# Routing attention and a bilinear feed-forward block: the preparation of the last twelve head pairs put across by VectorE in 32 by 32 blocks

## The chip, the cores and the metric

One core of one Trainium2 chip runs the whole kernel in one launch. The metric is the device time of one execution in microseconds; less is better. The kernel before takes 1099.45 us (median of 3 runs, 1099.21 to 1100.14).

## What is computed

```python
# q, k, v: (4, 8, 768, 64); centroids: (8, 16, 64)
q_assign = argmax(einsum('bhsd,hcd->bhsc', q_n, c_n), axis=-1)   # k_assign alike
mask = q_assign[:, :, :, None] == k_assign[:, :, None, :]
scores = where(mask, matmul(q, k.T) / 8, -1e9)
attn = exp(scores - max) / (sum + 1e-9)
x = matmul(attn, v)                      # heads side by side: (3072, 512)
out = ((x @ w_a) * (x @ w_b)) @ w_out    # d_ff = 1536
```

Every query and key row gets the nearest of 16 centroids of its head; a query attends to the keys of its own cluster. The result goes through a bilinear feed-forward block.

## The kernel before

The 4 batch elements x 8 heads are worked off as 16 **pairs** of heads, p = 0 to 15, four to a batch element. `HP` is 4, so pairs 4 to 15 are those of the last three batch elements. A pair takes six **groups** (l = 0 to 5) of the loop at L891, and the loop index is g = 6p + l. In each group TensorE issues, in this order:

1. `score` of the group's two units (L408): one-hot clusters against one-hot clusters (L416) and q against k (L425) into the PSUM tiles `s`; ScalarE takes the exponential (L432).
2. `weigh` of the group before (L451): probabilities against v (L457).
3. one step of the **preparation of the next pair** (`ready[l]()`, L907, from `prep_steps`, L380).
4. in every third group `denominators` (L480).
5. pieces of the feed-forward block of an earlier batch element (the queue `ffn`, L928 to L937), as many as a credit in columns allows. In the later batch elements these are products of the up projections (L639) and of the down projection (L758), most of them followed by one or two VectorE additions (L649, L764). After each piece one entry of the queue `todo` is issued, a VectorE operation of the preparation or of the normalization (L499 to L515). What is left in `todo` follows at the group's end (L941).

All these products, and all transposes of the preparation, take turns in three PSUM tiles named `m` (pool `ps_m`, L172).

The preparation of pair p+1, spread over the groups of pair p, is:

- l = 0 and the end of l = 0: TensorE turns q and k, 12 transposes of 128 x 128 (L308), so that the head dimension lies across partitions; ScalarE copies them out of PSUM in three copies of 128 x 512 (L316).
- l = 1: similarities to the centroids (L324), copied to SBUF by ScalarE (L329). v of the pair is loaded (L215).
- l = 2: TensorE turns the similarities (three transposes, L335); VectorE finds the first largest of 16 in five operations (L352 to L358) and leaves one-hot rows in bf16.
- l = 4 and its end: TensorE turns the one-hot rows (12 transposes in bf16, L368), and ScalarE copies them out of PSUM in two copies of 128 x 768 (L373, L378). For k the copy makes 0 and -2^60 of 1 and 0.

At the end of group l = 0 the next q and k are requested from HBM (`load(p + 2)`, L947) by four DMAs on the SP queue, in runs of 256 bytes (L189). The SP queue works in order. It also carries the loads of w_a, w_b and w_out (L239, in the first 296 us) and the stores of the result (L529).

In groups 0 to 41 VectorE, ScalarE and GpSimd round the weights from 64-bit words to float32 (`round_w`, L244): four VectorE operations of 128 x 512, one each on ScalarE and GpSimd, and a last one on VectorE (L275), some 36 times.

A second path of the program (`long_path`) is taken only for out-of-range data and does not run here.

## Time and profile before

| | |
|---|---|
| median of 3 runs | 1099.45 us |
| the profiled execution's own time | 1098.49 us |
| its span, first to last instruction | 1096.7 us |
| TensorE busy | 1076.1 us (98%), granted clock 0.998 on the mean |
| VectorE busy | 683.8 us (62%) |
| GpSimd busy | 331.0 us (30%) |
| ScalarE busy | 303.4 us (28%) |
| DMA | 64,247 packets, 45.00 MB |

The profile shows one execution. PE is TensorE, PEld its weight loads, DVE VectorE, ACT ScalarE, POOL GpSimd, SPq the DMA issues of the SP queue. A float32 matmul of the program stands in the trace as two passes, a transpose as one. Matmuls overlap in the pipeline, so the duration of one is longer than the step from its start to the start of the next; the cost of a group of matmuls is read from start to start.

### The profile page before, as it was taken

What the parts mean: (1) busy time and instruction counts of PE and PEld (TensorE: products, weight loads), DVE (VectorE), ACT (ScalarE), POOL (GpSimd) and SP (SyncE); (2) the same over time, 40 slices, a digit from 0 to 9 for tenths busy, and PEclk for the clock granted to TensorE, in tenths of its full rate; (3) what the DMA queues carried; (4) which work ended last, traced back from release to release, by engine and by line L of the source; (5) the groups of instructions that cost most, each with busy time, mean ns of one, the idle gap of its engine ahead of it and who ended that gap; (6) DMA issues with size and microseconds to landing.
All of it is one profiled execution on the core that took longest, in us unless ns stands there. A gap on an engine that the chain in (4) does not pass through costs nothing.

```text
span 1096.7 us, 13426 instructions
## 1 busy us (share of the span) xinstructions
PE 1076.1 (98%) x5043; PEld 629.1 (57%) x5043; DVE 683.8 (62%) x1346; ACT 303.4 (28%) x572; POOL 331.0 (30%) x317
## 2 busy tenths in 40 slices
PE   6999999999999999999999999999999999999998
PEld 3444445555556765555455767555555678555687
DVE  5888767576747337566664735666566655676662
ACT  4656424443331322232222222222231210000000
POOL 1111243443441323434343232234344320121200
PEclk9999999999999999999999999999999999999999
DMA  5333242324201020101001020010000001000001
GB/s 151 94 92 83 63 116 90 108 77 120 77 22 32 15 58 20 44 1 44 1 1 44 19 59 15 13 40 1 15 1 1 5 20 34 1 0 1 1 25 36
DMA packets 64247, 45.00 MB, mean 41 GB/s; under 512 B 48816, under 2 KB 59568, under 8 KB 64176
## 3 DMA queue, kind: packets, MB, share of 16 engines
q1 hardware_dynamic: 63200, 42.22, 13.6%
q10 hardware_dynamic: 976, 1.87, 0.5%
q8 instruction: 41, 0.67, 0.2%
q14 instruction: 30, 0.25, 0.1%
HBM read 37.78 MB, written 6.29 MB: 40 GB/s over the span
## 4 chain that ended last, share of the span: by engine, by line
PE 89%; DVE 5%; issue 4%; POOL 1%; ACT 0%; DMA 0%; DVEq 0%; POOLq 0%
PE m L639 30%; PE m L758 16%; PE O L457 11%; PE m L539 11%; PE s L425 10%; PE s L416 3%; PE m L480 3%; PE m L308 2%; PE m L324 1%; PE m L368 1%; DVE raw L600 1%; POOL acc L446 1%; PE m L335 1%; DVE xT L600 0%; DVE acc L446 0%
## 5 line engine op out<-in xcount | busy, mean ns | idle before, releaser
L432 ACT ACTIVATE pt<-s 128x768 f32<-128x768 f32 x192 | 145.5, 809 | 242.5 <-PE s L425 196.0
L446 POOL TENSOR_TENSOR acc<-acc,pt 128x384 f32<-128x384 f32 x144 | 149.4, 1051 | 65.1 <-ACT pt L432 48.2
L654 POOL TENSOR_TENSOR h<-h,ha 128x384 f32<-128x384 f32 x72 | 72.8, 1020 | 261.0 <-DVE ha L649 258.3
L457 PE MATMUL O<-pt,v 128*64 128x384 f32 x768 | 145.1, 499 | 0.0
L425 PE MATMUL s<-qkT 64*128 64x384 f32 x768 | 140.7, 486 | 0.0
L649 DVE TENSOR_TENSOR ha<-ha,m 128x384 f32<-128x384 f32 x126 | 67.1, 548 | 86.1 <-PE m L639 85.3
L649 DVE TENSOR_TENSOR h<-h,m 128x384 f32<-128x384 f32 x126 | 67.5, 549 | 79.4 <-PE m L639 78.9
L457 PEld LDWEIGHTS O<-pt,v 128*64 128x64 f32 x768 | 46.6, 136 | 86.4 <-issue 83.7
L512 POOL TENSOR_TENSOR xT<-xT,acc 128x384 f32<-128x384 f32 x32 | 33.3, 1039 | 197.8 <-DVE acc L507 167.5
L446 DVE TENSOR_TENSOR acc<-acc,pt 128x384 f32<-128x384 f32 x96 | 71.7, 776 | 30.1 <-POOL acc L446 29.7
L425 PEld LDWEIGHTS s<-qkT 64*128 64x128 f32 x768 | 71.1, 189 | 32.0 <-issue 0.8
L758 PE MATMUL m<-wo_sb,h 128*128 128x256 f32 x384 | 87.1, 381 | 0.0
L758 PEld LDWEIGHTS m<-wo_sb,h 128*128 128x128 f32 x384 | 72.2, 190 | 13.6 <-issue 1.8
L639 PE MATMUL m<-raw 128*128 128x384 f32 x192 | 70.0, 487 | 0.0
L539 PE MATMUL m<-xT,wb_sb 128*128 128x384 f32 x192 | 66.7, 491 | 1.9 <-DVE h L554 1.9
L539 PE MATMUL m<-xT,wa_sb 128*128 128x384 f32 x192 | 66.9, 492 | 0.0
L758 PE MATMUL m<-xT,h 128*128 128x256 f32 x288 | 65.3, 382 | 0.1
L758 PEld LDWEIGHTS m<-xT,h 128*128 128x128 f32 x288 | 54.1, 190 | 11.1 <-DVE acc L507 1.8
L639 PE MATMUL m<-xT,wa_sb 128*128 128x384 f32 x144 | 52.9, 490 | 0.0
L639 PE MATMUL m<-xT,size 128*128 128x384 f32 x144 | 52.6, 488 | 0.0
L639 PE MATMUL m<-xT,wb_sb 128*128 128x384 f32 x144 | 52.6, 488 | 0.0
L539 PEld LDWEIGHTS m<-xT,wb_sb 128*128 128x128 f32 x192 | 35.5, 190 | 28.9 <-DVE h L554 3.7
(149 smaller groups left out, 1501.2 us busy)
## 6 DMA issues: line engine op xcount, KB each, us to landing
raw<-in_moe_w_out_dram SPq DMA_DIRECT2D x12, 512.0 KB, 3.2
qk<-in_q_dram SPq DMA_DIRECT2D x30, 192.0 KB, 3.7
qk<-in_k_dram SPq DMA_DIRECT2D x30, 192.0 KB, 4.1
v<-in_v_dram SPq DMA_DIRECT2D x15, 384.0 KB, 4.3
raw<-in_moe_w_a_dram SPq DMA_DIRECT2D x11, 512.0 KB, 3.5
raw<-in_moe_w_b_dram SPq DMA_DIRECT2D x11, 512.0 KB, 3.5
out_dram<-rest SPq DMA_DIRECT2D x24, 128.0 KB, 1.7
out_dram<-comb SPq DMA_DIRECT2D x12, 128.0 KB, 1.7
```

The source lines that it names most:

```text
L416: nc.tensor.matmul(out=s[:, a, 0:HB], lhsT=ohTs[p][r, S + j * P:S + (j + 1) * P], rhs=ohTs[p][r, hf * HB:(hf + 1) * HB], start=True, stop= ...
L425: nc.tensor.matmul(out=s[:, a, 0:HB], lhsT=qkTs[p][r, S + j * P:S + (j + 1) * P], rhs=qkTs[p][r, hf * HB:(hf + 1) * HB], start=False, stop ...
L432: nc.scalar.activation(out=pt, in_=s[:, :, 0:HB], func=AF.Exp, scale=SCALE)
L446: eng.tensor_tensor(out=acc[:, a, :], in0=probs[u - 1][:, a, :] if j == 1 else acc[:, a, :], in1=probs[u][:, a, :], op=ALU.add)
L457: nc.tensor.matmul(out=O_of[0][a * D:(a + 1) * D, 0:HB], lhsT=vs[p][:, a, j, :], rhs=probs[u][:, a, :], start=(j == 0), stop=(j == NJ - 1))
L480: nc.tensor.matmul(out=ps[a * D:(a + 1) * D, 0:HB], lhsT=ones, rhs=t[:, a, :], start=(n == 0), stop=(n == len(terms) - 1))
L512: nc.gpsimd.tensor_tensor(out=x, in0=x, in1=den, op=ALU.mult)
L539: nc.tensor.matmul(out=ps[:, 0:HB], lhsT=w_sb[:, ch, f * P:(f + 1) * P], rhs=xTs[b][:, ch, t0:t0 + HB], start=(ch == 0), stop=(ch == NCH - 1))
L639: nc.tensor.matmul(out=ps[:, 0:HB], lhsT=A[l][c], rhs=rhs[c], start=(c == 0), stop=(c == 1))
L649: nc.vector.tensor_tensor(out=out, in0=in0, in1=ps, op=op)
L654: nc.gpsimd.tensor_tensor(out=to, in0=to, in1=box[name], op=ALU.mult)
L758: nc.tensor.matmul(out=ps[:, 0:HN], lhsT=A[l][f // 3][:, f % 3, :], rhs=B[r][f // 2][:, f % 2, :], start=(f == 0), stop=(f == N2 - 1))
```

## The change

For pairs 4 to 15 (`by_blocks(p)`: p >= 4) TensorE turns nothing any more. VectorE's `transpose` works on each block of 32 x 32 by itself. The loads lay q and k out for it: partition 32n + t of `qk` holds the 32 head-dimension elements of half n of token 32j + t (n counts two heads and two halves of the head dimension). Two VectorE transposes of 128 x 768 then give the same `qkT` as before. The similarities stay in PSUM until a VectorE transpose of 128 x 384 takes them across; queries then lie in partitions 0 to 63, keys in 64 to 127. The last step of the one-hot is split: VectorE compares the query half, GpSimd subtracts in the key half (which gives 0 and at most -2^60 directly). One VectorE transpose of 128 x 384 in bf16 takes both across, and eight small DMAs on the SP queue put the rows where `score` reads them. Tokens now lie in natural order, so v comes in two DMAs with runs of 256 bytes and the stores of these batch elements use another row order.

```diff
-    ohtp = pool("ohtp", 2)
+    ohtp = pool("ohtp", 1)
...
+    def by_blocks(p):
+        return p >= HP
+
     def load(p):
...
+        if by_blocks(p):
+            t = qkp.tile([P, 2, S // 32, 32], FP32, name="qk")
+            for w, src in enumerate((q, k)):
+                for n in range(4):
+                    a, d = divmod(n, 2)
+                    nc.sync.dma_start(
+                        out=t[32 * n:32 * n + 32, w],
+                        in_=src[b, 2 * hp + a, :, 32 * d:32 * d + 32].rearrange(
+                            "(j t) d -> t j d", t=32))
+            qks[p] = t
+            return
...
+        if by_blocks(p):
+            for a in range(2):
+                nc.sync.dma_start(
+                    out=t[:, a], in_=v[b, 2 * hp + a].rearrange(
+                        "(j p) d -> p j d", p=P))
+            return
...
+    ohT_bufs = [ohtp.tile([P, 2 * S], BF16, name=f"ohT{n}") for n in range(2)]
+
+    rank_far = zero.tile([P, NC], FP32, name="rank_far")
...
+        if by_blocks(p):
+            sims[p] = ps
+            return
         t = simp.tile([P, HB], FP32, name="sim")
         nc.scalar.copy(out=t, in_=ps[:, 0:HB])
         sims[p] = t
...
+    def prep_by_blocks(p):
...
+        def across(w):
+            v.transpose(out=qkTs[p][:, w * S:(w + 1) * S],
+                        in_=qks[p][:, w].rearrange("p j d -> p (j d)"))
+
+        def sims_across():
+            v.transpose(out=sim.rearrange("p g c -> p (g c)"),
+                        in_=sims[p][:, 0:HB])
+
+        def one_hot():
+            nc.gpsimd.tensor_tensor(out=oh[KT], in0=sim[KT], in1=top(first)[KT],
+                                    op=ALU.subtract)
+            v.tensor_tensor(out=oh[QT], in0=sim[QT], in1=top(first)[QT],
+                            op=ALU.is_equal)
+
+        def one_hot_across():
+            v.transpose(out=ohT, in_=oh.rearrange("p g c -> p (g c)"))
+            for a in range(2):
+                for kq in range(4):
+                    r = 32 * kq + a * NC
+                    nc.sync.dma_start(
+                        out=ohTs[p][a * D:a * D + NC, kq * HB:(kq + 1) * HB],
+                        in_=ohT[r:r + NC, :])
+
+        return [
+            [lambda: across(0), lambda: across(1)],
+            [sims_across],
+            [lambda: v.tensor_reduce(out=mx, in_=sim, axis=AX.X, op=ALU.max),
+             lambda: v.tensor_tensor(out=sim, in0=sim, in1=top(mx), op=ALU.is_ge),
+             lambda: v.tensor_tensor(
+                 out=sim, in0=sim, in1=rank_far[:, None, :].broadcast_to(shape),
+                 op=ALU.mult),
+             lambda: v.tensor_reduce(out=first, in_=sim, axis=AX.X, op=ALU.max)],
+            [one_hot],
+            [one_hot_across],
+            [],
+        ]
...
+        if by_blocks(p):
+            steps = prep_by_blocks(p)
+            ready = [lambda s=s: todo.extend(s) for s in steps]
+            ready[1] = both(lambda: prep_sim(p), lambda: load_v(p), ready[1])
+            return ready
...
+    for r, factor in ((slice(0, P // 2), 1.0), (slice(P // 2, P), FAR)):
+        nc.vector.tensor_scalar(out=rank_far[r], in0=rank[r], scalar1=factor,
+                                scalar2=None, op0=ALU.mult)
...
         if l == 0 and p + 1 < NPAIR:
-            prep_transpose(p + 1, 2)
+            if not by_blocks(p + 1):
+                prep_transpose(p + 1, 2)
             load(p + 2)
-        if l == 4 and p + 1 < NPAIR:
+        if l == 4 and p + 1 < NPAIR and not by_blocks(p + 1):
             prep_onehot(p + 1, 0)
```

The order of the instructions shows it at three places. First TensorE in group l = 0 of pair 11, where pair 12 is prepared. Before (`qk` are the loaded rows, `ident` the identity, `xT`, `raw`, `size` and `wa_sb` operands of up-projection products):

```order
L425 MATMUL s<-qkT 128x384 x4
L457 MATMUL O<-pt,v 64x384 x4
L308 MATMUL m<-ident,qk 128x128 x8
L639 MATMUL m<-xT,raw 128x384 x2
L639 MATMUL m<-xT,size 128x384 x2
L639 MATMUL m<-xT,wa_sb 128x384 x2
L639 MATMUL m<-raw 128x384 x2
L639 MATMUL m<-xT,wa_sb 128x384 x2
L308 MATMUL m<-ident,qk 128x128 x4
```

and now:

```order
L517 MATMUL s<-qkT 128x384 x4
L549 MATMUL O<-pt,v 64x384 x4
L732 MATMUL m<-xT,raw 128x384 x2
L732 MATMUL m<-xT,size 128x384 x2
L732 MATMUL m<-xT,wa_sb 128x384 x2
L732 MATMUL m<-raw 128x384 x2
L732 MATMUL m<-xT,wa_sb 128x384 x2
```

The twelve transposes are gone and the pieces follow each other directly; lines from L308 on have moved.

Second VectorE at the same place, groups l = 0 and l = 1 of pair 11. Before (L649 are the additions after a piece, L622 combinations of weights, L446 the sums of probabilities):

```order
L446 TENSOR_TENSOR acc<-acc,pt 128x384
L649 TENSOR_TENSOR ha<-ha,m 128x384 x3
L622 TENSOR_TENSOR raw<-wa_sb 128x128 x2
L622 TENSOR_TENSOR size<-wa_sb,raw 128x128 x2
L649 TENSOR_TENSOR h<-h,m 128x384 x2
L446 TENSOR_TENSOR acc<-pt 128x384
L649 TENSOR_TENSOR h<-h,m 128x384 x2
```

and now:

```order
L538 TENSOR_TENSOR acc<-acc,pt 128x384
L742 TENSOR_TENSOR ha<-ha,m 128x384 x2
L428 STREAM_TRANSPOSE qkT<-qk 128x768
L742 TENSOR_TENSOR ha<-ha,m 128x384
L428 STREAM_TRANSPOSE qkT<-qk 128x768
L715 TENSOR_TENSOR raw<-wa_sb 128x128 x2
L715 TENSOR_TENSOR size<-wa_sb,raw 128x128 x2
L742 TENSOR_TENSOR h<-h,m 128x384 x2
L538 TENSOR_TENSOR acc<-pt 128x384
L742 TENSOR_TENSOR h<-h,m 128x384
L432 STREAM_TRANSPOSE sim<-m 128x384
L742 TENSOR_TENSOR h<-h,m 128x384
```

Each transpose stands between the additions of two pieces.

Third the SP queue from group l = 0 of pair 5 on, where q and k of pair 7 and v of pair 6 are requested among the loads of weights. Before:

```order
L189 DMA qk<-in_q_dram 128x6x64 x2
L189 DMA qk<-in_k_dram 128x6x64 x2
L215 DMA v<-in_v_dram 128x2x384
L239 DMA raw<-in_moe_w_a_dram 128x512
L239 DMA raw<-in_moe_w_b_dram 128x512
L239 DMA raw<-in_moe_w_out_dram 128x512 x7
```

and now:

```order
L198 DMA qk<-in_q_dram 32x24x32 x4
L198 DMA qk<-in_k_dram 32x24x32 x4
L235 DMA v<-in_v_dram 128x6x64 x2
L263 DMA raw<-in_moe_w_a_dram 128x512
L263 DMA raw<-in_moe_w_b_dram 128x512
L263 DMA raw<-in_moe_w_out_dram 128x512 x4
L448 DMA ohT_171<-oh 16x384 x8
L263 DMA raw<-in_moe_w_out_dram 128x512 x3
```

Ten DMAs instead of five stand ahead of the next load of weights, and eight for the one-hot rows stand among the later ones.

## Rows read from the trace of the kernel before

**Rows 1.** The page, part 1: busy time of each engine.
```profile
PE 1076.1 (98%) x5043; PEld 629.1 (57%) x5043; DVE 683.8 (62%) x1346; ACT 303.4 (28%) x572; POOL 331.0 (30%) x317
```

**Rows 2.** The page, part 4: shares of the chain that ended last, by line.
```profile
PE m L639 30%; PE m L758 16%; PE O L457 11%; PE m L539 11%; PE s L425 10%; PE s L416 3%; PE m L480 3%; PE m L308 2%; PE m L324 1%; PE m L368 1%; DVE raw L600 1%; POOL acc L446 1%; PE m L335 1%; DVE xT L600 0%; DVE acc L446 0%
```

**Rows 3.** Busy time by stretch, the first 50 us (stretch, length, engines).
```profile
0.00:50.00 50.00, 39.09 (x247) 19.48 (x249) 32.92 (x71) 26.64 (x46) 7.71 (x13) 0.97 0.39 108
```

**Rows 4.** Timeline of PE, 568 to 621 us (start, length, engine, line, operation).
```profile
568.36 1.09 PE L308 MATMUL m<-ident,qk 128*128 128x128 f32 x8
569.28 1.46 PE L639 MATMUL m<-xT,raw 128*128 128x384 f32 x4
...
575.74 0.60 PE L308 MATMUL m<-ident,qk 128*128 128x128 f32 x4
576.27 0.50 PE L416 MATMUL s<-ohT 64*128 64x384 bf16 x4
...
590.82 0.55 PE L335 MATMUL m<-ident,sim 128*128 128x128 f32 x3
591.20 1.46 PE L639 MATMUL m<-raw 128*128 128x384 f32 x4
...
619.88 0.50 PE L368 MATMUL m<-identb,oh 128*128 128x128 bf16 x6
620.31 0.50 PE L416 MATMUL s<-ohT 64*128 64x384 bf16 x4
```

**Rows 5.** Groups by line and shape, DVE (count, busy us, mean ns, idle before).
```profile
L500 DVE STREAM_TRANSPOSE acc<-acc 128x384 f32<-128x384 f32 x32 | 18.2, 569 | 0.0
...
L354 DVE TENSOR_TENSOR sim<-sim,rank 128x384 f32<-128x384 f32 x16 | 10.1, 630 | 0.3
...
L732 DVE TENSOR_TENSOR xT<-wo_sb,xT 128x512 f32<-128x512 f32 x12 | 7.5, 679 | 0.0
```

**Rows 6.** Line L622 on DVE, 565 to 600 us (ns min/median/max).
```profile
L622 DVE TENSOR_TENSOR raw<-comb,wa_sb x2: 1085/1088/1092, 567.1 to 568.1; 128x128 f32<-128x128 f32 x2
...
L622 DVE TENSOR_TENSOR raw<-wb_sb x2: 282/283/284, 584.4 to 584.6; 128x128 f32<-128x128 f32 x2
```

**Rows 7.** Timelines of DVE and of POOL at 185 us.
```profile
185.20 0.57 DVE L500 STREAM_TRANSPOSE acc<-acc 128x384 f32<-128x384 f32 x1
...
185.36 1.27 POOL L268 TENSOR_TENSOR wb_sb<-wb_sb,rest 128x512 f32<-128x512 f32 x1 [3.35 <-DVE rest L263]
```

**Rows 8.** Waits, DVE for TensorE's up products (us in total, times, longest).
```profile
DVE ha L649 <- PE m L639: 85.3, 82, 4.5
```

**Rows 9.** A stretch of pair 3: busy time, and a row of PE's timeline.
```profile
109.00:122.00 13.00, 12.61 (x78) 5.68 (x75) 12.69 (x22) 8.34 (x15) 2.68 (x2) 1.00 0.14 45
...
111.67 1.01 PE L480 MATMUL m<-acc,ones 128*64 128x384 f32 x3 [0.39 <-DVE acc L446]
```

**Rows 10.** DMA of 320 to 340 us; timelines of SP and DVE; landing.
```profile
q1 hardware_dynamic: 3408, 1.18, 24.2%
...
202.43 1.25 SPq L189 DMA_DIRECT2D qk<-in_q_dram  x2
...
208.37 0.33 SPq L239 DMA_DIRECT2D raw<-in_moe_w_a_dram  x1
...
218.44 0.41 DVE L253 TENSOR_SCALAR wa_sb<-raw 128x512 int32<-128x512 int32 x1
...
raw<-in_moe_w_a_dram SPq DMA_DIRECT2D x11, 512.0 KB, 3.5
```

**Rows 11.** Timelines of DVE and PE at pair 11's end; the stores' issue and landing.
```profile
614.87 0.42 DVE L764 TENSOR_TENSOR ha<-comb,m 128x256 f32<-128x256 f32 x1 [1.60 <-PE m L758]
...
628.85 0.50 PE L416 MATMUL s<-ohT 64*128 64x384 bf16 x4
...
L529 SPq DMA_DIRECT2D out_dram<-rest x24: 332/332/362, 341.7 to 1089.4; - x24
...
DMA to landing us min/median/max: 1.7/1.7/2.9
```

More of the change, by code (lines that the diff above doesn't have):

```diff
@@ L213, in load_v @@
         t = vp.tile([P, 2, NJ, D], FP32, name="v")
+        vs[p] = t
+        if by_blocks(p):
[4 more added lines that the diff above has]
+            return
         eng = nc.scalar if p == 0 else nc.sync
@@ L217, in load_v @@
             in_=v[b, 2 * hp:2 * hp + 2].rearrange("a (p j) d -> p a (j d)", j=NJ))
-        vs[p] = t
     first = load_first()
@@ L362, in prep_onehot @@
     def prep_onehot(p, w):
-        if p not in ohTs:
-            ohTs[p] = ohtp.tile([P, 2 * S], BF16, name="ohT")
+        ohTs[p] = ohT_bufs[p % 2]
         ps = ps_m.tile([P, 1024], BF16, name="m")
@@ L378, in prep_onehot @@
             nc.scalar.copy(out=dst, in_=ps[:, 0:S])
+    def prep_by_blocks(p):
+        qkTs[p] = qtp.tile([P, 2 * S], FP32, name="qkT")
+        ohTs[p] = ohT_bufs[p % 2]
+        NG = 24
+        QT = slice(0, P // 2)
+        KT = slice(P // 2, P)
+        shape = (P, NG, NC)
+        sim = simp.tile([P, NG, NC], FP32, name="sim")
+        mx = small.tile([P, NG], FP32, name="mx")
+        first = small.tile([P, NG], FP32, name="first")
+        oh = oh_all[:, 0:3].rearrange("p n (g c) -> p (n g) c", c=NC)
+        ohT = oh_all[:, 3:6].rearrange("p n e -> p (n e)")
+        top = lambda t: t[:, :, None].broadcast_to(shape)
+        v = nc.vector
+        def across(w):
[30 more added lines that the diff above has]
+        ]
     def prep_steps(p):
@@ L526, in store @@
     def store(b, j, half, y):
-        rows = out[b * S:(b + 1) * S, :].rearrange(
-            "(p j) (half n) -> p j half n", j=NJ, half=2)
+        order = "(j p) (half n) -> p j half n" if by_blocks(b * HP) else \
+            "(p j) (half n) -> p j half n"
+        rows = out[b * S:(b + 1) * S, :].rearrange(order, j=NJ, half=2)
         nc.sync.dma_start(out=rows[:, j, half, :], in_=y)
```

## The prediction

> **What bounds the kernel now.** I read the page's busy shares first. TensorE is busy 1076.1 of 1096.7 us [rows 1], so it stands still for 20.6 us in all, and 10.9 of these lie in the first 50 us [rows 3], before there is anything to overlap. The chain of waits says the same: nearly every step is a matmul that followed another matmul, and the three transposing lines L308, L368 and L335 hold about 2%, 1% and 1% of it [rows 2]. So an instruction that leaves TensorE in the middle of the program shortens the program, as long as no other engine has to be waited for in its place. VectorE is the candidate for that: 62% on the whole span, but not evenly.
>
> **What leaves TensorE.** In the timeline I take steps from start to start for one prepared pair [rows 4]. Eight transposes of q and k: 569.28 - 568.36 = 0.92 us. The other four: 576.27 - 575.74 = 0.53. Three of the similarities: 591.20 - 590.82 = 0.38. Six of the one-hot rows: 620.31 - 619.88 = 0.43, and six more like them stand nine microseconds earlier, 0.43 again. The sum is 2.69, say 2.70 us per pair; twelve pairs are changed: **12 x 2.70 = 32.4 us**. The order agrees: TensorE's list has lost these rows, and the feed-forward pieces and scores stand where they stood.
>
> **What leaves ScalarE**: three copies, the similarity copy and two one-hot copies per pair. ScalarE is busy 28% [rows 1] and TensorE seldom waits for it, so I cost this at nothing.
>
> **What VectorE gets.** A transpose of 128 x 384 takes 0.57 us [rows 5]. One of 128 x 768 is not in the trace. Its lower bound comes from the growth with width: 128 x 512 takes 0.679 [rows 5] and 128 x 128 undisturbed 0.283 [rows 6], which is 1.03 ns an element, so 0.57 + 384 x 1.03 ns = 0.97 us. Its upper bound is twice the narrow one, 1.14. I take 0.97, because the same kind of operation with a fixed part is the nearer row. Per pair: 2 x 0.97 + 0.57 (similarities) + 0.57 (one-hot, upper end; bf16 may be quicker) = 3.08 us. The comparison that now reads two SBUF tiles instead of PSUM and SBUF is like L354, 0.63 us [rows 5], some 0.08 more. That is 12 x 3.2 = 38 us, and VectorE goes from 684 to about 722 us, 68% of the shorter span. The two tiny operations at the start lie where VectorE waits for TensorE: nothing.
>
> Is it hidden? In group l = 0 each transpose follows a piece. The five pieces between 569.28 and 575.74 [rows 4] take 1.29 us each; VectorE then has 0.55 for the addition and 0.97 for the transpose, 1.52. It falls 0.23 behind twice, 0.46 in all, which three `m` tiles can carry, and it stood waiting for TensorE's up products for 85.3 us in one of the two groups of these additions alone [rows 8]. At l = 1 the similarities hold one `m` tile for about one piece longer, since VectorE frees it and not ScalarE; the other two alternate. I expect no wait there. Lower bound of what these eleven pairs lose: 0. Upper bound: all of VectorE's addition on the path, 11 x 3.2 = 35 us. I take 0.14 us each, **1.5 us**, near the lower end because of the waits of rows 8.
>
> Pair 3, where pair 4 is prepared, is different. There VectorE also rounds weights and does all sums: from 109 to 122 us it is busy 12.69 of 13 us, and TensorE waits 0.39 us for its sums [rows 9]. This pair can lose between nothing and its whole 2.7 us. Two of the new transposes, 2 x 0.57, fall at this place, and 0.31 of the 13 us are free: 0.8, with the wait for the similarities that now stands in VectorE's queue I take **1.0 us**.
>
> A VectorE operation beside GpSimd can be held up: L622 takes 1.09 us where POOL adds and 0.28 where it does not [rows 6]. A transpose is not: at 185.20 us it takes its 0.57 with POOL running through nearly all of it [rows 7]. The Trainium skill has this in "SBUF — State Buffer", "SBUF: two separate sides": a GpSimd operation, or a VectorE operation that reads two SBUF tensors, has the shared port pair for its whole length and the other waits. Rows 6 against rows 7 agree with both halves of it. By that rule the comparison that now reads SBUF twice could wait a whole POOL operation each time, 12 x 1 us more on VectorE, and the sum on TensorE would stay, since that is no more than the waits of rows 8.
>
> **GpSimd** gets one half-height subtraction per pair, about 1 us by its other operations, at 30% load: nothing. VectorE's one-hot transpose, which waits for it, is a whole group later.
>
> **The queues.** Per pair SP issues 8 + 2 DMAs for q, k and v instead of 4 + 1, and 8 small ones. q, k are due a pair later, some 60 us, and v too. Transfers: 3408 packets took 24.2% of 20 us on all 16 engines, 4.84 us [rows 10]. Now there are 6144 of 128 bytes and 1536 of 256: at the same time per packet (they are no larger) 10.9 us. What stands behind them are the loads of weights, in pairs 4 to 6. q starts at 202.43, the load behind at 208.37, it takes 3.5 to land and is used at 218.44 [rows 10]. Eight issues at 0.62 and two for v at as much make 6.2 us, so that load would start at about 209 and, behind transfers that end at 202.4 + 10.9 = 213.3, land by 217. Just in time: I take 0, upper bound in the second rival. The one-hot rows: VectorE's transpose can follow the addition that ends at 615.3 and is done by 615.9; eight issues of 0.33 and a landing of 1.7 [rows 11] make 620.3, and the score that needs them starts at 628.85, or 628 now. Hidden by 7.7 us. Stores have the same size.
>
> **Sum.** 1098.49 (the profiled execution's own time) - 32.4 + 1.5 + 1.0 = 1068.6 us. The median of the runs is 0.96 us above this execution, so I forecast **1069.5 us**. A measurement here can tell about 0.2% (2.2 us) from no change.
>
> **Rivals.**
>
> *VectorE late in every pair.* If transposes cost their upper 1.14 us and meet combinations of weights of 1.09 us an operation [rows 6], VectorE is a full piece behind, the three `m` tiles are used up, and TensorE waits about one addition and one transpose less a piece's slack, some 1.1 us, in each of eleven pairs: 12 us, **1081.5 us**. For it: those combinations stand right behind the second transpose in the order. Against it: VectorE's waits for TensorE [rows 8]. Chance 0.10.
>
> *Loads of weights late.* If a packet of 128 bytes takes twice as long, 7680 packets need 21.8 us, the load of weights behind them lands near 227 and not by 218.44, 9 us late, in three pairs. VectorE's order is fixed, so its feed-forward additions wait too; three `m` tiles cover some 4 us: 3 x 5 = 15 us, **1084.5 us**. Against it: that the packets of 256 bytes in rows 10 already go at 22.7 ns each on an engine. The Trainium skill speaks for it, in "DMA: Bandwidth & Descriptors", Specifications: transfers under 512 bytes are read-modify-written and miss line rate; both sizes fall under it, and no row here has packets of 128 bytes. Chance 0.06.
>
> *One-hot rows late at the next pair's score* (the slower side). The eight DMAs hang on VectorE, and on SP they are behind stores. If each lands only after the one before, at the 3.5 us of a load of weights [rows 10], the last is there 28 us after 615.9, 16 us after the score wants it, twelve times: 1069.5 + 192 = **1261 us**. It turns into a loss when the landing takes more than the 12.1 us there are plus the 2.7 that the pair saves. Against it: 1.7 us landing, issues that overlap. Chance 0.03.
>
> *The gain does not come* because TensorE was only filling time that VectorE or the exponentials set anyway: within 2 us of **1099**. Against it: rows 1 and 8. Chance 0.02.
>
> **Numbers.** My forecast, with losses of 0 to 7 us in place of 2.5, has 0.79 and reaches from 1067 to 1074. The low end of the range lies 2 us lower, for stalls of TensorE that vanish and steps that are longer in other pairs. The high end takes in the first rival: 1065 to 1082. Faster by over 0.2%: 0.79 + 0.10 + 0.06 = 0.95; same 0.02; slower 0.03.
>
> **What would show it.** Right: no matmul of the transposing lines after 100 us; TensorE busy near 1046 and still idle for some 20 to 25 us; VectorE near 722 us; the new transposes of 128 x 768 at 0.97 us; no wait of the one-hot matmuls on a DMA. Wrong: waits of TensorE for the new transposes or for additions at l = 0 or 1 (first rival), of VectorE's rounding for a DMA between 140 and 280 us (second), of L508 for a DMA (third).

## The result, and the profile after

The changed kernel takes 1073.83 us (median; 1072.50 to 1074.87), the kernel before in the same comparison 1099.42 us: a ratio of 0.9765 with a 95% interval of 0.9748 to 0.9782. The forecast was 1069.5 us, in a range of 1065 to 1082. The direction and the mechanism were right; 4.3 us of the expected gain are missing, and most of this part is about where they went.

The page of the changed kernel first, part 1 (busy time, share of the span, instructions) and the line of part 4 that gives the shares of the chain by line:

```profile
PE 1046.6 (98%) x4719; PEld 602.5 (56%) x4719; DVE 713.7 (67%) x1396; ACT 259.0 (24%) x500; POOL 355.8 (33%) x329
...
PE m L732 30%; PE m L851 19%; PE O L549 12%; PE m L632 12%; PE s L517 11%; PE s L508 4%; PE m L572 3%; PE m L353 1%; DVE raw L693 1%; PE m L337 1%; DVE raw L715 1%; DVE xT L693 0%; DVE acc L538 0%; PE m L399 0%; DVE size L693 0%
```

(Lines have moved: L308 is now L337, L457 is L549, L639 is L732, L758 is L851, L622 is L715, L600 is L693, L446 is L538, L480 is L572, L649 is L742, L764 is L857.) TensorE is busy for 29.5 us less than in [rows 1], and the profiled span, 1071.4 us, is 25.3 us shorter. The idle time of TensorE has grown, from 20.6 to 24.8 us.

The timeline of PE where the first four of [rows 4] stood, the group l = 0 of one pair:

```profile
549.65 1.56 PE L732 MATMUL m<-xT,raw 128*128 128x384 f32 x4
551.04 1.45 PE L732 MATMUL m<-xT,size 128*128 128x384 f32 x4
...
554.91 1.45 PE L732 MATMUL m<-xT,wa_sb 128*128 128x384 f32 x4
556.30 0.50 PE L508 MATMUL s<-ohT 64*128 64x384 bf16 x4
```

No transpose stands between the products any more, and TensorE does not stop where they stood. But the neighbours have become longer. The first piece now takes 551.04 - 549.65 = 1.39 us from start to start; behind the transposes the step to the next piece was 1.30 us in the kernel before (569.28 to 570.58 us in its timeline). The last piece, from which the scores now follow at once, takes 556.30 - 554.91 = 1.39 as well, against 1.29 (574.45 to 575.74).

The waits of TensorE in the changed kernel, all but the start and the smallest (us in total, times, longest):

```profile
PE m L732 <- DVE comb L715: 4.8, 3, 2.2
PE m L399 <- DVE oh L390: 3.2, 1, 3.2
PE m L572 <- DVE acc L538: 2.3, 4, 1.1
PE m L732 <- DVE ha L742: 0.9, 2, 0.4
```

VectorE's new operations, by groups of line and shape (count, busy us, mean ns, idle time before them):

```profile
L428 DVE STREAM_TRANSPOSE qkT<-qk 128x768 f32<-128x768 f32 x24 | 22.8, 963 | 0.0
...
L432 DVE STREAM_TRANSPOSE sim<-m 128x384 f32<-128x384 f32 x12 | 6.9, 576 | 1.8 <-PE m L353 1.8
L444 DVE STREAM_TRANSPOSE oh<-oh 128x384 bf16<-128x384 bf16 x12 | 6.8, 570 | 0.0
L440 DVE TENSOR_TENSOR oh<-sim,first 64x384 bf16<-64x384 f32 x12 | 6.5, 546 | 0.0
```

SP's issues of the one-hot rows, 96 of them (fewest, median and most ns, first and last start), and the time from issue to landing:

```profile
L448 SPq DMA_DIRECT2D ohT<-oh x96: 512/587/1692, 118.0 to 792.6; - x96
...
DMA to landing us min/median/max: 1.7/1.8/4.1
```

The wide transposes cost what was forecast, 0.96 us, and no one-hot matmul waits for a DMA. New are the waits of L732 for L715 and L742: 4.8 and 0.9 us. (L399 belongs to pair 0 and is as before.) They lie at l = 4 of pairs 8 and 12 and at l = 3 of pairs 10 and 14, in the steps that make the one-hot rows (the third and smallest wait for L715, 0.4 us behind the last pair, is as before), and not at l = 0 or 1, where the prediction looked for them.

At pairs 8 and 12 the kernel before had a wait at this place already, 0.47 us each time. Its timeline of PE at pair 8:

```profile
425.10 1.56 PE L639 MATMUL m<-raw,comb 128*128 128x384 f32 x4 [0.47 <-DVE comb L622]
```

So VectorE's chain was the longer one there before anything was changed, and no row of the prediction shows it.

**The account, group by group.** In all these kernels TensorE starts the products with v (L549, output O) once in each of the 96 groups, in the same order. The step from one start to the next, in the kernel before minus in the changed one, tells what each group gained. Away from the events named below these steps agree between executions to 0.02 us, and the second profiled execution of the changed kernel (below) has the same steps throughout.

| what | where | us |
|---|---|---|
| q and k transposes gone, l = 0 | 1.76 in pair 3, 1.61 in pair 4 (read from the kernel with q and k alone, below), 1.27 in each of pairs 5 to 14 | +16.0 |
| similarity transposes gone, l = 2 | 0.47 in pair 3, 0.53 in pairs 4 to 6, 0.28 in pairs 7 to 14 | +4.3 |
| one-hot transposes gone, l = 4 | 0.78 in pair 3, 0.93 in eleven pairs | +11.0 |
| a wait of the kernel before that is gone, pair 4 | L539 for VectorE's h, at 160 us | +1.9 |
| pair 3: the sums of l = 3 | L572 for VectorE's acc | -0.7 |
| pair 4, first group | L572 for VectorE's acc: 1.03 gained in place of 1.61 | -0.6 |
| pairs 8 and 12, l = 4 | L732 for L715, with the combination of x (L693) in front; 0.1 in the next group | -3.6 |
| pairs 10 and 14, l = 3 | L732 for L742 | -1.3 |
| sum | first to last O: 868.09 us before, 841.03 after, difference 27.06 | 27.0 |

The wait in pair 4 is no idle time in the rows, since earlier products still count as busy; but the trace has VectorE's last sum of L538 end at 130.75 us (130.20 + 0.55) and the product that needs it start 0.06 us later, while in the kernel with q and k alone that sum is done 1.9 us before the products.

Outside that stretch 0.9 us are lost in the first 24 us and 0.8 after the last store's issue: 27.06 - 0.92 - 0.83 = 25.3, the difference of the spans.

### The profile page after: what moved, and what is told of

It is laid out like the page before. It is cut to its first block, busy times and chain, and to the rows that moved or that the text cites. A ratio compares the mean times of both kernels' runs of the same rounds, so it can differ in the third digit from the quotient of the medians.

```text
span 1071.4 us, 13000 instructions
## 1 busy us (share of the span) xinstructions
PE 1046.6 (98%) x4719; PEld 602.5 (56%) x4719; DVE 713.7 (67%) x1396; ACT 259.0 (24%) x500; POOL 355.8 (33%) x329
## 4 chain that ended last, share of the span: by engine, by line
PE 93%; DVE 5%; issue 0%; DMA 0%; POOL 0%; ACT 0%; DVEq 0%; POOLq 0%
PE m L732 30%; PE m L851 19%; PE O L549 12%; PE m L632 12%; PE s L517 11%; PE s L508 4%; PE m L572 3%; PE m L353 1%; DVE raw L693 1%; PE m L337 1%; DVE raw L715 1%; DVE xT L693 0%; DVE acc L538 0%; PE m L399 0%; DVE size L693 0%
## 5 line engine op out<-in xcount | busy, mean ns | idle before, releaser
L538 POOL TENSOR_TENSOR acc<-acc,pt 128x384 f32<-128x384 f32 x144 | 151.9, 1068 | 59.8 <-ACT pt L524 43.5
L549 PE MATMUL O<-pt,v 128*64 128x384 f32 x768 | 145.1, 499 | 0.0
L742 DVE TENSOR_TENSOR ha<-ha,m 128x384 f32<-128x384 f32 x126 | 66.8, 546 | 74.1 <-PE m L732 73.3
L742 DVE TENSOR_TENSOR h<-h,m 128x384 f32<-128x384 f32 x126 | 67.4, 549 | 68.5 <-PE m L732 67.7
L538 DVE TENSOR_TENSOR acc<-acc,pt 128x384 f32<-128x384 f32 x96 | 72.8, 787 | 35.4 <-POOL acc L538 35.0
L549 PEld LDWEIGHTS O<-pt,v 128*64 128x64 f32 x768 | 46.6, 136 | 86.4 <-issue 82.1
L851 PE MATMUL m<-wo_sb,h 128*128 128x256 f32 x384 | 87.5, 382 | 0.0
L851 PEld LDWEIGHTS m<-wo_sb,h 128*128 128x128 f32 x384 | 72.1, 190 | 16.0 <-issue 4.2
L732 PE MATMUL m<-raw 128*128 128x384 f32 x192 | 70.2, 488 | 0.9 <-DVE ha L742 0.9
L851 PE MATMUL m<-xT,h 128*128 128x256 f32 x288 | 65.4, 382 | 0.1
L851 PEld LDWEIGHTS m<-xT,h 128*128 128x128 f32 x288 | 54.1, 190 | 11.7 <-issue 1.7
L732 PE MATMUL m<-xT,wa_sb 128*128 128x384 f32 x144 | 53.0, 491 | 0.0
L732 PE MATMUL m<-xT,size 128*128 128x384 f32 x144 | 52.9, 490 | 0.0
L732 PE MATMUL m<-xT,wb_sb 128*128 128x384 f32 x144 | 52.9, 490 | 0.0
L632 PEld LDWEIGHTS m<-xT,wa_sb 128*128 128x128 f32 x192 | 35.5, 190 | 29.4 <-issue 3.6
```

Source lines behind the costliest of these rows:

```text
L538: eng.tensor_tensor(out=acc[:, a, :], in0=probs[u - 1][:, a, :] if j == 1 else acc[:, a, :], in1=probs[u][:, a, :], op=ALU.add)
L549: nc.tensor.matmul(out=O_of[0][a * D:(a + 1) * D, 0:HB], lhsT=vs[p][:, a, j, :], rhs=probs[u][:, a, :], start=(j == 0), stop=(j == NJ - 1))
L632: nc.tensor.matmul(out=ps[:, 0:HB], lhsT=w_sb[:, ch, f * P:(f + 1) * P], rhs=xTs[b][:, ch, t0:t0 + HB], start=(ch == 0), stop=(ch == NCH - 1))
L732: nc.tensor.matmul(out=ps[:, 0:HB], lhsT=A[l][c], rhs=rhs[c], start=(c == 0), stop=(c == 1))
L742: nc.vector.tensor_tensor(out=out, in0=in0, in1=ps, op=op)
L851: nc.tensor.matmul(out=ps[:, 0:HN], lhsT=A[l][f // 3][:, f % 3, :], rhs=B[r][f // 2][:, f % 2, :], start=(f == 0), stop=(f == N2 - 1))
```

## The experiments

**The changed kernel again.** Nothing is edited.

> The changed kernel as it is, once more. It tells whether the two differences at the ends (0.92 us lost before 25 us, where the granted clock was lower than in the kernel before, and 0.84 us after the last product) belong to the change or to one execution. If they belong to one execution, the profile's span varies by about 1 us between executions of the same kernel and the median stays at 1073.8 within 0.5.

Median 1072.99 us (ratio to the kernel before 0.9758, 0.9744 to 0.9771), span 1072.7. From the first O to the last it takes 841.02 us, against 841.03: the middle of the program is the same to the hundredth. The first O starts at 25.08 us, against 23.83, and that is the whole difference of the spans, 1.3 us. Over fourteen profiled executions of these kernels, whose first part is nearly the same, the first O starts between 22.9 and 25.1 us; the kernel before had 22.91, at the early end. So the 0.9 us at the start belong to the execution. The end does not: from the last store's issue to the end of the span it is 5.3 to 5.7 us in all twelve executions with the changed order of stores, and 4.7 and 4.2 in the two with the old order (the kernel before, and the one with the rows alone). About 1 us goes with that order. Why is not shown.

From here on "the stretch" is the time from the first O to the last, which these differences at the ends don't touch.

**One half of the change, then the other.**

```
e1: ready[0] = across as in the change; similarities and one-hot rows
    as in the kernel before (prep_across, prep_assign, prep_onehot)
e2: ready[0] = prep_transpose(p, 0), (p, 1); loads, v and stores as in the
    kernel before; similarities and one-hot rows as in the change
```

> Only q and k are put across by VectorE (new loads, natural token order for v and the stores); similarities and one-hot rows stay on TensorE as in the kernel before. Theory A, VectorE is late in four groups only: twelve transposes give TensorE back 1.27 us in each of the 12 pairs (read from the changed kernel's trace), 15.2 us, and the four groups that wait in the changed kernel (two with the combination of x, two at l = 3) do not wait here, since their one-hot comparison and transpose are not on VectorE. 1099.4 - 15.2 = 1084.2, range 1082.5 to 1085.5. Theory B, the lost time is spread over all pairs because the transposes of 128 x 768 make VectorE late at l = 0: the shortfall of about 6 us stays in this kernel, about 1088 to 1090. The prediction's own term (1.45 us a pair) would give 1082.

> Only the similarities and the one-hot rows are put across by VectorE and the small transfers; q and k are loaded and transposed by TensorE as before. Theory A: 0.92 us for the one-hot rows in 12 pairs, 0.53 for the similarities in three and 0.28 in nine make 15.1 us; the four groups that wait in the changed kernel (2 x 1.73 and 2 x 0.65, 4.8 us) wait here too: 1099.4 - 10.3 = 1089.1, range 1087.5 to 1090.5, and the gains of this kernel and of the one with q and k alone add up to the whole change. Theory B (the shortfall belongs to the wide transposes): the whole 15.1 us comes, 1084.3.

q and k alone: 1085.77 us (ratio 0.9871, 0.9854 to 0.9887), stretch 853.27, 14.8 us shorter than before. The similarities and rows alone: 1089.73 us (0.9909, 0.9892 to 0.9925), stretch 858.08, 10.0 us shorter. Both fell near where theory A put them (15.2 and 10.3 expected; the first median is 0.3 us above its range). All four late waits, and pair 3's, stand in the second kernel at the same size and are missing from the first, whose waits for L715 are as before (1.3 us in three). TensorE's waits in the kernel with the rows alone:

```profile
PE m L731 <- DVE comb L714: 4.8, 3, 2.2
...
PE m L572 <- DVE acc L538: 2.2, 4, 1.1
PE m L731 <- DVE ha L741: 0.9, 2, 0.4
```

And in the kernel with q and k alone:

```profile
PE m L632 <- DVE h L647: 1.9, 1, 1.9
PE m L572 <- DVE acc L538: 1.6, 4, 0.4
PE m L732 <- DVE comb L715: 1.3, 3, 0.5
```

So the wide transposes of q and k, which the prediction feared, make no such wait by themselves, and the small one-hot steps, which it cost at nothing, make all four. The old wait of 1.9 us in pair 4 is still there with q and k alone: the other half removes it. The timelines suggest how. In the kernel before, the similarities lie in one of the three `m` tiles until VectorE's L352 and L353 read them at 158.99 and 159.92 us, and the group's fourth product waits until 160.06 for VectorE's L554, which frees another of the tiles; in the changed kernel VectorE takes them out at 144.97, before the group's products begin, and the fourth follows at once (155.33). No run moves that one step alone. The two halves add up to 24.8 us, 2.2 less than the whole. 1.6 of that is one event in the second kernel (the clock, at the end of this document), 1.2 are two waits of the first in pairs 5 and 6 that the whole change does not have, and 0.6 work the other way, the loss of pair 4, which neither half has alone.

**Twice the wide transposes.**

```
         def across(w):
+            for _ in range(2):
                 v.transpose(out=qkTs[p][...], in_=qks[p][:, w]...)
```

> Each transpose of q and k by VectorE is done twice: 24 more operations of 0.97 us, 23.3 us more on VectorE. Theory A, they are hidden: only pair 3, where VectorE has no room, shows its 1.9 us, and in the others a group with two pairs of them falls 2.4 us behind, which three m tiles can just carry: 1075 to 1079. Theory B, VectorE's list sets the pace at l = 0 in every pair: 12 x 1.94 = 23 us, 1094 to 1097.

1077.40 us (0.9794, 0.9777 to 0.9810), stretch 844.97: 3.9 us lost for 21.4 us more on VectorE (735.1 us busy against 713.7). Theory A held in size. It was wrong on the place: pair 3 lost 0.1, pairs 5 and 6 lost 1.4 and 2.0, where the similarities' matmul waits for the transposes and VectorE still rounds weights, and pair 10 lost 0.4. The wait of the similarities' matmul, from TensorE's waits, which names 1.6 of these 3.4 us:

```profile
PE m L353 <- DVE qkT L429: 1.6, 2, 1.0
```

**Half the packet, twice the packets and twice the issues.** Each load of q and k is cut in two.

```
+    for e in range(0, 32, 16):
         nc.sync.dma_start(out=t[32 * n:32 * n + 32, w, :, e:e + 16],
                           in_=src[b, 2 * hp + a, :, 32 * d + e:32 * d + e + 16]...)
```

> The loads of q and k are cut in two along the 32 columns of a block: 16 transfers a pair in place of 8, 64 bytes a packet in place of 128, the same bytes and twice the packets. Theory A, transfers are hidden and the packets' size costs nothing on the path: within 1.5 us of 1073.8. The prediction's second rival, loads of weights that stand behind these come late in pairs 4 to 6: VectorE's rounding waits for a DMA between 140 and 280 us and the time is 1078 to 1089.

1076.60 us (0.9795, 0.9779 to 0.9811), stretch 843.85: 2.8 us lost, between the two figures expected. 1.64 of that is the clock again, at pair 8, far from any of these loads. The other 1.2 us are pair 6, and there the sign that the prediction had named for its second rival appears. The waits of VectorE between 140 and 300 us:

```profile
DVE wo_sb L279 <- DMA raw<-in_moe_w_out_dram: 2.2, 1, 2.2
...
DVE wa_sb L279 <- DMA raw<-in_moe_w_a_dram: 1.1, 1, 1.1
```

In the changed kernel there is no such wait. But what makes these loads late is mostly not the packets. SP issues the load of w_a behind q, k and v; first in the changed kernel, then in this one:

```profile
203.69 0.64 SPq L263 DMA_DIRECT2D raw<-in_moe_w_a_dram  x1
208.26 0.73 SPq L265 DMA_DIRECT2D raw<-in_moe_w_a_dram  x1
```

The first issue of q stands at 197.85 and 198.14 us, so the load of w_a is issued 5.8 us behind it in the changed kernel and 10.1 here: eight more issues, of 0.52 us at the median. From issue to landing it takes 4.7 and 5.1 us. Of the 4.7 us by which it lands later, 4.3 are SP's issues and 0.4 the transfer. Around this load a packet of 128 bytes took 13.5 ns of a DMA engine on the mean, one of 64 bytes 10.2. So the margin for the loads of weights is used up by twice the issues; no run changes the packets alone. The Trainium skill warns of transfers below 512 bytes in "DMA: Bandwidth & Descriptors", Specifications. The packets agree, as half the bytes take three quarters of the time, but that is not what delayed the load.

**One-hot steps a group earlier.** A transpose at l = 4 stands in VectorE's list between the combination of x and the additions that TensorE waits for. This edit takes it away.

```
-             lambda: v.tensor_reduce(out=first, ...)],
-            [one_hot], [one_hot_across], [],
+             lambda: v.tensor_reduce(out=first, ...), one_hot],
+            [one_hot_across], [], [],
```

> The one-hot comparison goes from l = 3 to the end of l = 2, and the one-hot transpose with its eight small transfers from l = 4 to l = 3, so that no such transpose stands in VectorE's list in front of the combinations at l = 4. Theory A, the chain of VectorE's operations sets the pace in the two groups with the combination of x: each wait of 2.20 us gets shorter by the transpose's 0.57, 1.1 us in all, and the two waits at l = 3 stay about as they are: 1072 to 1073, against 1073.8. Rival, the wait is there because TensorE no longer has the one-hot transposes to do and the combination of x alone sets the pace: less than 0.5 us, and the waits stay at 2.2.

1080.16 us (0.9819, 0.9806 to 0.9833): slower than the changed kernel by 6 to 7 us, against either theory. The stretch is 847.10. Step by step both are visible: the waits of 2.20 became 1.68, each group gaining 0.52, as theory A said, and those at l = 3 vanished, 0.56 each. But 2.8 us were lost in pair 3, of which 0.6 came back in pair 4's first group, and 1.0, 2.4, 1.7 and 0.9 in pairs 5, 6, 7 and 11. There TensorE waits for qkT in pair 6 (L353, 1.45 us) and for VectorE's combinations for the down projection in pairs 7 and 11 (L852 for L826, 1.50 and 0.27).

Pair 3 shows two causes at once. The timeline of PE there:

```profile
111.85 1.37 PE L573 MATMUL m<-acc,ones 128*64 128x384 f32 x3 [2.31 <-DVE acc L539]
```

The stretches around it (length, busy time of the engines in the page's order; third from the end is the granted clock):

```profile
109.00:112.00 3.00, 0.69 (x5) 0.15 (x2) 2.93 (x5) 0.54 (x2) 1.12 (x1) 1.00 0.74 156
112.00:115.00 3.00, 3.00 (x8) 0.98 (x7) 2.90 (x7) 0.00 (x0) 0.34 (x1) 0.54 0.00 0
115.00:118.00 3.00, 3.00 (x19) 1.50 (x20) 2.97 (x6) 2.57 (x5) 0.93 (x1) 0.89 0.25 38
```

The wait has grown from 1.08 to 2.31 us, and VectorE is busy for 2.93 of the 3 us there. Each half of the one-hot step has a part in it: in the two kernels below, which move one half each, pair 3 loses 0.58 and 0.64 us. Behind the wait of 2.31 us the clock is granted at 0.54, nearly all at the lower level of 1.2 GHz, which takes the other 1.6 us. For the rest a look at VectorE's waits for GpSimd's additions gave a lead: 35.0 us in 20 waits in the changed kernel, 51.9 in 28 here.

**Which half of the one-hot step.** The step is a comparison on VectorE and a subtraction on GpSimd. Two kernels move one each.

```
e8: [..., equal], [minus], [one_hot_across], []
e9: [..., minus], [equal], [one_hot_across], []
```

> Only VectorE's half of the one-hot step, the comparison, goes from l = 3 to l = 2; GpSimd's subtraction stays at l = 3 and the transpose at l = 4. It splits what the kernel with both moved earlier lost (6.1 us between the first and the last product with v, 847.1 us against 841.0 of the changed kernel). Theory C, that kernel lost because GpSimd's subtraction then stood in front of GpSimd's own additions, for which VectorE waits (51.9 us in 28 waits against 35.0 in 20): here nothing of that is lost; the two waits at l = 3 go (2 x 0.56 gained), the waits of 2.20 stay, and pair 3, where VectorE is full, loses 0.6, or 2.8 if the clock falls behind its wait: 840.5 to 842.7 for the stretch, time 1072.5 to 1075. Theory D, it lost because VectorE has no room for the comparison at l = 2 in pairs 4 to 7: 845 to 847, time 1077 to 1079.

> Only GpSimd's half, the subtraction, goes from l = 3 to l = 2; VectorE's comparison stays at l = 3 and the transpose at l = 4. Theory C (GpSimd's order is what hurt): the losses of the kernel with both moved at pairs 5, 6, 7 and 11 (1.03, 2.37, 1.71 and 0.89) come here too: 846 to 847 us from the first to the last product with v, time 1078 to 1079, and VectorE waits near 52 us for GpSimd's additions. Theory D (VectorE's list is what hurt): 841.0, time 1073, and some 35 us of such waits.

VectorE's half early: 1073.85 us (0.9762, 0.9748 to 0.9775), stretch 840.97, as the changed kernel. GpSimd's half early: 1079.70 us (0.9816, 0.9803 to 0.9830), stretch 847.41. That is theory C in the main: pairs 5, 6 and 7 lose 0.96, 2.79 and 1.40 us with GpSimd's half early, and 0.20 in all with VectorE's. Pair 11 does not belong to it, since it loses with either half (0.60 with VectorE's, 0.96 with GpSimd's). Of the second's 6.4 us, 1.6 are the clock behind a wait in pair 8. In the changed kernel, VectorE's waits for GpSimd's additions, and the waits of GpSimd's subtraction:

```profile
DVE acc L538 <- POOL acc L538: 35.0, 20, 2.4
...
POOL oh L438 <- DVE first L460: 26.3, 5, 6.0
```

With VectorE's half early:

```profile
DVE acc L539 <- POOL acc L539: 33.2, 18, 2.3
```

With GpSimd's half early:

```profile
DVE acc L539 <- POOL acc L539: 54.2, 28, 3.1
...
POOL oh L436 <- DVE first L460: 63.8, 8, 17.6
```

GpSimd works in the order of its list. At l = 2 the subtraction stands in front of GpSimd's additions and waits for VectorE's `first`, 63.8 us in all; the additions wait behind it, and VectorE then waits for the additions. GpSimd's timeline in pair 4, group l = 2, in the changed kernel, where the additions come first:

```profile
158.16 3.97 POOL L538 TENSOR_TENSOR acc<-acc,pt 128x384 f32<-128x384 f32 x3
```

and with GpSimd's half early:

```profile
159.41 0.84 POOL L436 TENSOR_TENSOR oh<-sim,first 64x384 bf16<-64x384 f32 x1 [2.08 <-DVE first L460]
160.33 3.23 POOL L539 TENSOR_TENSOR acc<-acc,pt 128x384 f32<-128x384 f32 x3
```

The additions start 2.2 us later. Such a delay reaches TensorE where VectorE has no slack: up to pair 6 it still rounds weights and has little. So what the unmoved order does is keep the subtraction behind the additions. Why pairs 7 and 11, where no weights are rounded, lose too was not followed beyond the wait for L826.

**The combination of x in two halves.**

```
-    ffn.insert(len(ffn) - FREE_ROOM, (0, lambda: combine_x(b)))
+    ffn.insert(len(ffn) - FREE_ROOM, (0, lambda: combine_x(b, 0)))
+    ffn.insert(len(ffn) - FREE_ROOM + 1, (0, lambda: combine_x(b, 1)))
```

> The eight subtractions that combine x run in two halves of four, with one product's piece and its addition between them, in place of eight in a row. Theory A (the eight in a row, with the transpose behind them, hold back the next addition and so TensorE): the two waits of 2.20 us shrink to between 0 and 1 us: 2.4 to 4.4 us less, 1069.5 to 1071.5. Rival (the sum of VectorE's work in these groups sets the pace, its order does not): within 0.5 us of 1073.8, with the wait a piece later.

> Both: one-hot steps one group earlier, and the combination of x in two halves. Theory A: the two waits of 2.20 us nearly vanish, 1069 to 1071, and the gains of the two single edits do not add up in full, since they take the same wait away. Rival (a sum of VectorE's work that no order changes): only the one-hot move counts, about 1072.7.

No effect: 1074.10 us (0.9763, 0.9750 to 0.9776), stretch 841.03, the waits again 2.20. Together with the early steps 1078.69 us (0.9813, 0.9799 to 0.9826), stretch 847.01, as with these alone. My theory A of this run fell: the order of these eight subtractions does not matter, since TensorE waits for the last link (L715), behind all of them. Only taking work out of that chain helps.

**Early only where it helps.** The early steps for four pairs, whose groups had gained.

```
+        ] if p not in (9, 11, 13, 15) else [
+            ..., one_hot], [one_hot_across], [], []]
```

> The one-hot steps go a group earlier for the pairs 9, 11, 13 and 15 alone, those whose preparation falls on a wait of the changed kernel (the combination of x at l = 4, twice; l = 3, twice) and on no group that the early steps hurt. Group by group the kernel with all of them early gained 0.52, 0.56, 0.52 and 0.56 there, 2.16 us: 838.9 us from the first to the last product with v against 841.0, and a time of 1070.8 against 1073.0. Rival, the groups are not independent (what VectorE saves in one group it loses in the next): within 0.5 us of 841.0.

1071.48 us (0.9744, 0.9731 to 0.9758), stretch 839.21: 1.8 of the 2.16 us, 0.53, 0.21, 0.52 and 0.55 in the four groups. Only pair 10's falls short. So the groups are independent but for that one.

**The combination of x without GpSimd beside it.** The changed kernel's timeline of VectorE at pair 8:

```profile
401.74 1.35 DVE L693 TENSOR_TENSOR raw<-xT 128x384 f32<-128x384 f32 x1
403.13 1.24 DVE L693 TENSOR_TENSOR xT<-xT 128x384 f32<-128x384 f32 x1
...
405.67 1.24 DVE L693 TENSOR_TENSOR size<-raw,xT 128x384 f32<-128x384 f32 x1
406.83 0.55 DVE L693 TENSOR_TENSOR raw<-xT 128x384 f32<-128x384 f32 x1
...
409.07 0.57 DVE L444 STREAM_TRANSPOSE oh<-oh 128x384 bf16<-128x384 bf16 x1
...
410.60 0.49 DVE L715 TENSOR_TENSOR comb<-raw,wa_sb 128x128 f32<-128x128 f32 x2
```

GpSimd's additions there:

```profile
402.64 3.85 POOL L538 TENSOR_TENSOR acc<-acc,pt 128x384 f32<-128x384 f32 x3
```

And TensorE's wait:

```profile
410.94 1.24 PE L732 MATMUL m<-raw,comb 128*128 128x384 f32 x3 [2.20 <-DVE comb L715]
```

Four subtractions of two SBUF tensors take more than twice as long as the four behind them, and they end with GpSimd's additions. The edit, on top of the last kernel, gives these three additions to VectorE, in two groups (units 104, 105, 152, 153):

```
-            many = p >= HP and (a == 1 or j in (2, 4))
+            many = p >= HP and (a == 1 or j in (2, 4)) and u not in ALONE
```

> As the kernel with the one-hot steps of pairs 9, 11, 13 and 15 a group earlier, and three additions of GpSimd are given to VectorE in each of the two groups with the combination of x; they come behind that combination in VectorE's list, where it waits for TensorE. Theory E, the combination is slow because GpSimd adds beside it: in the changed kernel the first four of its eight subtractions take 1.35, 1.24, 1.23 and 1.24 us while GpSimd runs these additions, the last four 0.55 to 0.56 without. Three of the four are then quick, 2.0 us less in a chain for which TensorE still waits 1.7: both waits go, up to 3.4 us less, 836 us from the first to the last product with v against 839.2, and a time near 1068.3. Rival, the sum of VectorE's work between two waits sets the pace, wherever the additions stand: 2.0 saved and 1.4 (3 x 0.47) added, 838 and 1070.3. Rival, the four are slow for another reason (what they read): the waits stay at 1.7 and the stretch at 839.2 or above.

1068.55 us (0.9714, 0.9701 to 0.9727), stretch 835.51, as theory E said (836). VectorE's timeline:

```profile
401.78 1.36 DVE L708 TENSOR_TENSOR raw<-xT 128x384 f32<-128x384 f32 x1
403.17 0.56 DVE L708 TENSOR_TENSOR xT<-xT 128x384 f32<-128x384 f32 x1
```

TensorE's waits for L730 and L757, which are L715 and L742 of the changed kernel:

```profile
PE m L747 <- DVE comb L730: 0.4, 1, 0.4
PE m L747 <- DVE ha L757: 0.2, 1, 0.2
```

The first subtraction still meets the one addition that stayed on GpSimd; the next three are quick, and both waits are gone. VectorE runs six operations more and is still busy no longer than in the kernel before this edit (714.8 us against 715.7), and the stretch is 3.7 us shorter. The Trainium skill has the mechanism in "SBUF — State Buffer", "SBUF: two separate sides": a VectorE operation with two SBUF inputs and a GpSimd operation hold the shared ports in turn, each for a whole instruction. The trace agrees: 1.24 us beside, 0.56 alone, and the changed kernel's transposes, with one input, take 0.57 and 0.94 to 0.97 us whether GpSimd runs beside them or not. This is the best version: 31 us under the kernel before, and 5.5 under the changed one in the stretch (4.4 and 5.3 by its two medians).

## Why the prediction was right, and where it was wrong

- **Right: what leaves TensorE shortens the program.** It is the bound for nearly all of the span. Of the 32.4 us, 31.3 came.
- **Mis-sized: 2.70 us per pair.** It measured 2.5 in pairs 7 to 14, 2.7 in pairs 5 and 6 and some 3.0 in pairs 3 and 4: mostly 1.27 for q and k against 1.45, 0.28 for the similarities (0.5 in four pairs) against 0.38, 0.93 for the one-hot rows against 0.86. I took a removed group's step from its start to the next start. The neighbours' steps change by about 0.1 us when another kind of product follows, 1.39 in place of 1.29, and each border counts. That accounts for q and k (2 x 0.1 of the 0.18); for the other two the steps were not followed. Cost: 1.1 us.
- **Right: VectorE's price.** 0.96 us for 128 x 768 (0.97 taken), 0.57 each for the others. VectorE is busy for 713.7 us, not 722. The comparison that now reads two SBUF tiles (L456) costs 0.55 at the median and 0.63 on the mean, as taken, so it explains at most 1 of these 8 us. The combinations of weights (L622, now L715) got some 5 us shorter in all; the rest was not followed.
- **The step that failed: "the eleven pairs lose 1.5 us".** They lost 5.5, and pair 3 0.7 (1.0 taken). The doubled transposes show that l = 0 and 1, which I had worked through, were nearly as free as I said (pair 4's first group, 0.6 us, is the exception). I had not worked through l = 3 and 4, where the comparison and the one-hot transpose go; they were "hidden" only by VectorE's waits for TensorE as a sum over the run [rows 8]. In four groups VectorE's own chain is the longer one. At l = 4 of pairs 8 and 12 the removed 0.93 us of TensorE turned into a wait, with 0.8 us of VectorE's additions on top; at l = 3 of pairs 10 and 14 TensorE had lost no work, and the comparison alone made the loss of 0.65 us. The waits of 0.47 us for L622 in the kernel before were the sign of it at pairs 8 and 12. The slow subtractions that make two of these chains long were the L622 pattern of [rows 6] on another line; I used that row for a rival at l = 0 and did not look for the same thing at l = 4.
- **Not foreseen: the vanished wait**, 1.9 us to the good, which is luck: without it the forecast would have been 6.2 us off. With q and k alone it stays, with the other half it goes; the similarities that leave their `m` tile earlier are the likely reason. The prediction looked at that tile only at l = 1, where it is held longer, and not at l = 2, where the similarities no longer take one.
- **Queues: right in effect, wrong in numbers.** Issues of the small transfers take 0.59 us and not 0.33, landing 1.8 against 1.7, and the score never waits. The 22.7 ns a packet from [rows 10] had the larger packets of v in it; packets of 128 bytes took 13.5 ns, so the 6144 of q and k take 5.2 us on 16 engines. The loads of weights were in time; with eight more issues in front of them they no longer are.
- **Stores of the same size at nothing:** about 1 us at the end goes with their new order.

In the sum: 1.1 (size) + 3.7 (waits: 5.5 + 0.7 in place of 1.5 + 1.0) - 1.9 (vanished) + 0.8 (end) make 3.7 of the 4.3 us; the remaining 0.6 lies within what the first 24 us vary by between executions.

The first rival (VectorE late in every pair) did not come: the waits stand in four groups and in pairs 3 and 4. The sign of the second came only with the loads cut in two, and then by SP's issues and not by the time of a packet, as the rival had it. The third had no trace, and the fourth fell with the gain of 25.6 us.

## What to carry to other kernels

Where one engine is the bound, moved work is paid for only in the groups where the receiving engine's own chain is the longer one: look for these group by group, above all where a rare step (here the combination of x) lands, and not by the sum of its waits. A short wait that is there before the change, such as the 0.47 us here, marks such a group. An operation on an engine that works in order must not stand in front of another engine's inputs: a subtraction moved one group forward on GpSimd cost 6.4 us, 1.6 of them by the clock, with no more work anywhere. And before an operation is called slow, see what ran beside it: three additions moved off GpSimd in each of two groups were worth 3.7 us.

## What the runs showed of the hardware

- **A wait can cost more than itself.** Behind a wait of 1.08 us (pair 3, changed kernel) the granted clock stayed at 1.00, behind 2.31 us in the same pair (the kernels with the whole one-hot step early) it fell to the lower level. Behind the same wait of 2.1 to 2.2 us at pair 8 it fell in three of eight profiled executions and not in the others, for 1.6 us each time; at pair 12 it fell in none. The stretches of the kernel with halved loads, where it fell at pair 8:

```profile
409.00:412.00 3.00, 1.25 (x4) 0.38 (x2) 2.93 (x8) 0.48 (x1) 0.00 (x0) 1.00 0.00 0
412.00:415.00 3.00, 2.55 (x10) 1.17 (x12) 1.88 (x9) 0.00 (x0) 0.00 (x0) 0.74 0.09 21
415.00:418.00 3.00, 3.00 (x15) 1.32 (x13) 0.54 (x2) 1.33 (x2) 0.00 (x0) 0.69 0.05 13
```

And of the changed kernel, where it did not:

```profile
408.00:411.00 3.00, 0.80 (x4) 0.19 (x2) 2.96 (x9) 0.48 (x1) 0.00 (x0) 1.00 0.02 4
411.00:414.00 3.00, 3.00 (x16) 1.46 (x16) 1.92 (x7) 0.33 (x1) 0.00 (x0) 1.00 0.09 22
```

- The first 24 us vary by up to 2.2 us between the fourteen executions, whose instructions there are nearly the same, and by 1.25 us between the two of the changed kernel. The granted clock between 12 and 24 us differs with it: 1.00, 0.69, 0.74 and 1.00 in stretches of 3 us in the kernel before, 1.00, 0.58, 0.50 and 0.78 in the changed kernel's second execution.
- A GpSimd operation beside a run of two-input VectorE operations can be reported very long. The subtraction, 0.97 us at its quickest and 1.19 at the median, took 7.00 at 584.23 us in the changed kernel, while VectorE ran such operations back to back until 590.45; VectorE's own took 0.54 to 0.67 each there but for the first, 1.35. Nothing waited for it. Spans on GpSimd are rough, so the number is only what GpSimd's timeline reports:

```profile
584.23 7.00 POOL L438 TENSOR_TENSOR oh<-sim,first 64x384 bf16<-64x384 f32 x1
```
